# Gated linear attention followed by a ReLU-squared MLP: q loaded for two chunks at a time, scores of two chunks together, sixteen output tiles stored late

## The chip, the cores and the metric

The kernel runs on one core of a Trainium2 chip (trn2). The metric is device time in microseconds (us) of one execution; for the kernel before it is the median of three runs. A profile of one further execution gives the durations. "The span" is the time from the first to the last instruction in that profile; the execution's own time is a little longer.

## The reference

Four sequences of 768 tokens, eight heads of 48 channels. For each head a 48x48 state decays by a gate per channel and gains one outer product per token; the result of the attention, 3,072 tokens of 384 channels, goes through a two-layer MLP with 2,048 hidden units.

```python
for t in range(S):
    state = alpha[:, :, t, :, None] * state + np.einsum('bhd,bhe->bhde', k[:, :, t], v[:, :, t])
    y[:, :, t] = np.einsum('bhd,bhde->bhe', q[:, :, t], state)
x = y.transpose(0, 2, 1, 3).reshape(B * S, H * D)
h = x @ w_in
g = np.maximum(h, 0.0) ** 2
return g @ w_out
```

q, k, v, alpha and the weights come as fp32 in HBM, the output goes back as fp32. The matmuls take bf16 operands.

## The kernel before, in words

**Chunks.** The 3,072 tokens are cut into 24 chunks of 128 (six for each sequence). A chunk's tokens stand on the 128 partitions. Within a chunk the recurrence becomes matrix products: the logarithm of alpha is summed along the tokens by a matmul with a triangular matrix (`e_p0`, L428, and for its transpose `e_pT`, L444), exps of the sum and of its negative scale q and k, and the scores k·q are masked with a triangle (`e_sm`, L558) and multiplied with v (`e_p3b`, L595). The state of the chunks before enters by `e_p3a` (L589), and is brought up to date by `e_ps` and `e_stm` (L567, L579). The result of a chunk, cast to `xn` (L608), is transposed into `xT_big` (L231), either on TensorE (`e_p4`) or, for chunks 18 to 22 (`XTURN`, L313), by a DMA transpose (L620).

**Two ways to q and k.** Up to chunk 10, q and k are scaled on VectorE in their own layout and transposed on TensorE (`e_p1q`, `e_p1k`). From chunk `RAW` = 11 on (L312), POOL casts q and k to bf16 (`e_rb`, L411), a DMA transpose on SP's queue turns each (`e_turn`, L415), the cumulated gate is made in transposed form (`e_pT`), and VectorE multiplies the two (`e_qAT`, `e_kiT`, L506 and L509).

**Scores.** `e_p2` (L549) issues eight matmuls for a chunk. Each contracts over 64 rows (a head's 48 channels, padded), so that two of them, on the upper and the lower 64 rows of the array, stand side by side. They write the two banks of PSUM of the pool `ps_sc`.

**Banks.** PSUM's other banks are five single-bank pools, `sl_bank`. The attention takes turns on the first two (`GLA_BANKS`), the MLP on the others.

**MLP.** `add_moe1` (L652) multiplies groups of one to four token tiles with w_in; ScalarE takes the ReLU, VectorE the square. `add_moe2` (L725) multiplies one tile of 128 tokens with w_out; ScalarE or VectorE copies the result out of PSUM, and a DMA stores it. The last tile goes in two halves of 192 columns (`add_last`, L691).

**Stores.** Tiles 0 to 7 (`HELD` = 8, L644) are copied into two tiles of four (`KEEP`) and stored from SP's queue not before 150 us of the plan, four tiles in one DMA (L763). Tiles 8 to 17 are stored from POOL's queue as they are made (`POOL_OUT`, L643), tiles 18 to 23 from SP's (L772, L721). A token tile's store writes 128 consecutive rows of 1,536 bytes in HBM.

**What sets the order.** Nothing is ordered by hand: class `Plan` (L59) simulates all engines with a cost and a priority for each operation before the program is emitted, and each engine then gets its instructions in the order of the planned starts. DMAs on SP's queue are part of it (`DMA` for loads, `TR` for DMA transposes, `OUT` for stores). A gate (L836) lets chunk s begin when s is at most `LEAD` = 3.7 plus the number of tiles that the MLP has done.

**Loads.** One DMA for each of q, k, v and alpha of a chunk (L371); a token of one head is 48 fp32 numbers, so that every contiguous piece in HBM is 192 bytes. The alphas of the first four chunks come together, four tokens per partition (L336).

Of the kernel before, what the change touches and what calls it, by code (L numbers as in the profile page):

```python
# [38 lines left out]
class Op:  # L39


    def __init__(self, eng, dur, emit, deps=(), prio=0.0, takes=None, gives=None, lat=None, at=0.0):
        self.eng, self.dur, self.emit = eng, dur, emit
        self.deps = []
        for d in deps:
            if d is not None:
                d = d if isinstance(d, tuple) else (d, None)
                if d[0] is not None:
                    self.deps.append(d)
        self.prio = prio  # L50
        self.takes, self.gives, self.lat, self.at = takes, gives, lat, at
        self.start = self.done = None
# [6 lines left out]
class Plan:  # L59
# [13 lines left out]
    def ready(self, op):  # L73
        t = op.at
        slack = PE_SLACK if "PE" in op.durs else 0.0
        if slack and self.free.get("PE", 0.0) > PE_CALM:
            slack = 0.25
        for d, x in op.deps:
            if d.done is None:
                return None  # L80
            if x is None:
                t = max(t, d.done + (slack if d.eng != "PE" else 0.0))
            else:
                t = max(t, d.start + d.dur + x)
        if op.takes is not None:
            best = None
            for sl in op.takes:
                f = sl.free_at()
                if f is not None and (best is None or f < best):
                    best, op.slot = f, sl  # L90
            if best is None:
                return None
            t = max(t, best)
        return t

    def run(self, gate):
        free = self.free
        while any(self.pending.values()):
# [34 lines left out]
            if op.takes is not None:  # L133
                self.ready(op)
                op.slot.release.append(op.gives if op.gives is not None else op)
            self.order.append(op)
# [5 lines left out]
def kernel(  # L142
# [27 lines left out]
    out_r = out.rearrange("(tt p) n -> tt p n", p=P)  # L170

# [26 lines left out]
    nc.gpsimd.tensor_copy(utri_b[:, 0, :], utri_f)  # L198
    JN, JP = 4, 32
# [31 lines left out]
    xT_big = big.tile([P, KT, n_tok], BF16)  # L231
# [80 lines left out]
    RAW = 11  # L312
    XTURN = (18, 23)  # L313
    TLD, TLAT, TLATE = 1.0, 4.0, 2.0
# [3 lines left out]
    def raw_tiles():  # L318
        if R:
            return  # L320
        R["b"] = stage.tile([P, NR, 2, H, DP], BF16, name="rawb", tag="stage")
        nc.gpsimd.memset(R["b"][:, :, :, :, D:], 0.0)
        R["t"] = stage.tile([P, NR, 2, NP, P], BF16, name="rawt", tag="stage")
        R["i"] = stage.tile([P, 2, NP, P], BF16, name="aiT", tag="stage")
# [39 lines left out]
    def add_load(s, nm):  # L364
        d = C[s]
        b, c = divmod(s, NCH)

        def ld():
            if nm not in d:
                d[nm] = loads.tile([P, H, D], FP32, name=nm)  # L370
            pin(nc.sync.dma_start(out=d[nm], in_=SRC[nm][b, c]))  # L371
        prev = C[s - LB].get("use_" + nm) if s >= LB else None
        d["ld_" + nm] = add("DMA", LD if s < 4 else LD1, ld, prev, lat=2.0 if s < 4 else LAG if s < 6 else 2.4, at=0.6)

    def add_chunk(s):
        d = C[s]
# [31 lines left out]
        if raw:  # L408
            w, wz = s % NR, s % 2

            def e_rb(j, nm):  # L411
                raw_tiles()
                pin(nc.gpsimd.tensor_copy(R["b"][:, w, j, :, 0:D], d[nm]))  # L413

            def e_turn(j):  # L415
                pin(nc.sync.dma_start_transpose(out=R["t"][:, w, j], in_=R["b"][:, w, j].rearrange("p h d -> p (h d)")))
            rt = []
            for j, nm in enumerate(["qt", "kt"]):
                cb = add("POOL", 0.55, lambda j=j, nm=nm: e_rb(j, nm), d["ld_" + nm],
                         *([C[s - NR]["turn"][j]] if s >= RAW + NR else []), prio=-5.0)  # L420
                d["use_" + nm] = cb
                t_ = add("TR", TLD, lambda j=j: e_turn(j), cb, *([C[s - NR]["turned"][j]] if s >= RAW + NR else []), lat=TLAT)
                t_.late = TLATE
                rt.append(t_)
            d["turn"] = rt
# [23 lines left out]
        def e_AT():  # L449
            d["qkT"] = work.tile([P, 2 * NP, P], BF16, name="qkT")  # L450
            pin(nc.scalar.activation(d["qkT"][:, NP:2 * NP, :], d["pmT"], AF.Exp))  # L451
# [26 lines left out]
        if raw:  # L478
# [10 lines left out]
            pT.gives = aiT  # L489
            if not last:  # L490
# [15 lines left out]
        def e_qAT():  # L506
            pin(nc.vector.tensor_mul(d["qkT"][:, 0:NP, :], R["t"][:, w, 0], d["qkT"][:, NP:2 * NP, :]))

        def e_kiT():  # L509
            pin(nc.vector.tensor_mul(d["qkT"][:, NP:2 * NP, :], R["t"][:, w, 1], R["i"][:, wz]))  # L510
        if raw:
            if not last:
                mk = d["use_kt"] = add("DVE", 0.47, e_kI, ai, d["ld_kt"], old, **g)
            cp = add("DVE", 0.34, e_qAT, aT, rt[0], **g)
            cpk = add("DVE", 0.34, e_kiT, aiT, rt[1], cp, **g)
            d["turned"] = [cp, cpk]
        else:
            mq = d["use_qt"] = add("DVE", 0.47, e_qA, a_, d["ld_qt"], old, **g)
            mk = d["use_kt"] = add("DVE", 0.47, e_kI, ai, d["ld_kt"], old, **g)

# [28 lines left out]
        def e_p2():  # L549
            sc = d["sc"] = ps_sc.tile([P, 2, NP, P], FP32, name="sc")  # L550
            t = d["qkT"]
            for p in range(NP):
                for hh in range(2):
                    sl = slice(64 * hh, 64 * hh + 64)
                    mm(sc[:, hh, p, :], lhsT=t[sl, NP + p, :], rhs=t[sl, p, :], start=True, stop=True)
        p2 = d["p2"] = plan.add(Op("PE", 0.42, e_p2, [cp, cpk], takes=[sl_sc], lat=0.10, **g))

        def e_sm(hh):  # L558
            if hh == 0:
                d["sm"] = work.tile([P, 2, NP, P], BF16, name="sm")  # L560
            pin(nc.vector.tensor_mul(d["sm"][:, hh], d["sc"][:, hh], utri_b.to_broadcast([P, NP, P])))  # L561
        sm0 = add("DVE", 0.6, lambda: e_sm(0), p2, **g)
        sm1 = add("DVE", 0.6, lambda: e_sm(1), p2, after(sm0), **g)
        p2.gives = sm1

# [52 lines left out]
        if XTURN[0] <= s < XTURN[1]:  # L618
            def e_xt():
                pin(nc.sync.dma_start_transpose(out=xT_big[:, :, s * P:(s + 1) * P], in_=d["xn"]))  # L620
# [6 lines left out]
        def e_xT():  # L627
            cast(xT, xT_big[:, :, s * P:(s + 1) * P], d["px"])
# [15 lines left out]
    HELD, HELD_AT = 8, 150.0  # L644
# [7 lines left out]
    def add_moe1(g, f0, before, lo=0, hi=None, per=1):  # L652
        hi = GN[g] if hi is None else hi
        t0, n = (GT[g] + lo) * P, (hi - lo) * P
# [36 lines left out]
    def add_last(g, tt, before, pools):  # L691
# [3 lines left out]
        for hf in range(2):  # L695
# [24 lines left out]
            def e_out(box=box, cols=cols):  # L720
                pin(nc.sync.dma_start(out=out_r[t][:, cols], in_=box["ob"]))  # L721
# [3 lines left out]
    def add_moe2(g, tt, before, box, quarters, pools):  # L725
# [22 lines left out]
        def e_ev():  # L748
            if held:
                if t % 4 == 0:  # L750
                    KEEP[t // 4] = stage.tile([P, 4, d_model], FP32, name="keep", tag="stage")
# [10 lines left out]
        def e_held():  # L762
            pin(nc.sync.dma_start(out=out_r[t - 3:t + 1].rearrange("t p n -> p t n"), in_=KEEP[t // 4]))  # L763
        if held:
            held_ev.append(ev)
            if t % 4 == 3:
                add("OUT", 2.2, e_held, *held_ev[-4:], at=HELD_AT)
            return op

        def e_out():  # L770
            dma = nc.gpsimd if pool_out else nc.sync
            pin(dma.dma_start(out=out_r[GT[g] + tt], in_=box["ob"]))  # L772
# [61 lines left out]
    LEAD = 3.7  # L834

    def gate(op):  # L836
        s = getattr(op, "gla", None)
        if s is not None:
            return s <= LEAD + (prog["m1"] + prog["m2"]) / 5.12
# [61 lines left out]
```

## Time and profile before

| | |
|---|---|
| median of three runs | 184.71 us (184.2 to 185.06) |
| the profiled execution | 185.07 us |
| its span in the profile | 183.4 us |
| TensorE busy | 177.5 us in 1,908 matmuls |
| VectorE, ScalarE busy | 127.1 us, 126.5 us |
| DMA packets | 120,200, of which 112,400 under 512 bytes |
| read from and written to HBM | 25.17 MB, 4.72 MB |

A line of the page's fifth part gives a group of like instructions: source line, engine, operation, result <- operands, shape, count, then busy time and the mean of one in ns, then the idle time of the engine just ahead of them and what ended it. PE is TensorE's matmuls, PEld its weight loads, DVE VectorE, ACT ScalarE, POOL GpSimd, SP the engine whose queue issues most DMAs. All `mm` calls have line 240 and all PE transposes line 243, so that they are told apart by the names of their tiles: `sc` are the scores, `st` the state. A matmul's listed duration includes its way through the array; how fast matmuls follow one another is read from the starts.

### The profile page before, as it was taken

Reading aid. Unit: us, or ns where it says so; the run is one execution under the profiler, and the core shown is the slowest. Engines: PE = TensorE matmul, PEld = TensorE weight load, DVE = VectorE, ACT = ScalarE, POOL = GpSimd, SP = SyncE. Lnnn points to the kernel's source line nnn. Section 1 sums busy time; section 2 is a strip of 40 time slices with the busy share of each in tenths; the row PEclk is TensorE's granted clock in tenths of the full one; section 3 lists DMA queues with packets and bytes.
Section 4 is the critical chain, followed back from the end, with each engine's and each line's share of the span. In section 5 each row is a group of like instructions: output and inputs, shape, how many; then the busy total and the mean of one; then the engine's idle time right before and its main releaser. Section 6 shows DMA issues by size and latency. Waiting matters only on the chain.

```text
span 183.4 us, 4946 instructions
## 1 busy us (share of the span) xinstructions
PE 177.5 (97%) x1908; PEld 130.5 (71%) x1908; DVE 127.1 (69%) x273; ACT 126.5 (69%) x286; POOL 39.4 (21%) x80
## 2 busy tenths in 40 slices
PE   7999999899999999999999998999999999999993
PEld 2577884567769877867768776667766777778663
DVE  1179898684999998778877867748855984744200
ACT  3677799226859996966967859847975895767321
POOL 8221100021131142132223133342323512000000
PEclk9999999999999999999999999999999999999999
DMA  5999999999999999998999599898898898901022
GB/s 168 215 212 252 302 366 321 326 220 204 177 191 201 194 179 173 141 190 161 150 193 202 113 240 186 161 227 162 170 201 182 176 163 194 301 13 43 12 77 86
DMA packets 120200, 34.12 MB, mean 186 GB/s; under 512 B 112400, under 2 KB 118928, under 8 KB 120176
## 3 DMA queue, kind: packets, MB, share of 16 engines
q1 hardware_dynamic: 119536, 31.83, 80.7%
q0 software_dynamic: 640, 1.97, 3.2%
q8 instruction: 15, 0.25, 0.6%
q14 instruction: 9, 0.07, 0.2%
HBM read 25.17 MB, written 4.72 MB: 163 GB/s over the span
## 4 chain that ended last, share of the span: by engine, by line
PE 49%; DMA 2%; ACT 1%; issue 0%; DVE 0%
PE bank L240 45%; DMA at<-in_alpha_dram 2%; PE sc L240 2%; PE st L240 1%; PE bank L243 1%; ACT aiT L454 0%; ACT r L676 0%; ACT ob L758 0%; ACT L_s L396 0%; ACT ob L716 0%; DVE xT_big L388 0%; ACT qkT L451 0%
## 5 line engine op out<-in xcount | busy, mean ns | idle before, releaser
L240 PE MATMUL bank<-xT_big,w_in_b 128*128 128x256 bf16 (+2 forms) x636 | 76.6, 262 | 0.9 <-ACT r L676 0.7
L240 PE MATMUL bank<-w_out_b,gT 128*128 128x384 bf16 (+1 forms) x400 | 71.6, 320 | 0.5 <-DVE w_out_b L296 0.5
L676 ACT ACTIVATE r<-bank 128x512 bf16<-128x512 f32 x96 | 56.6, 606 | 11.3 <-PE bank L240 9.9
L240 PEld LDWEIGHTS <-w_in_b 128*128 128x128 bf16 x636 | 52.7, 98 | 10.6 <-issue 1.5
L240 PEld LDWEIGHTS <-gT 128*128 128x128 bf16 x416 | 37.2, 98 | 18.7 <-DVE w_out_b L296 1.0
L684 DVE TENSOR_TENSOR gT<-r 128x512 bf16<-128x512 bf16 x96 | 41.8, 453 | 10.2 <-ACT r L676 9.0
L561 DVE TENSOR_TENSOR sm<-sc,utri_b 128x512 bf16<-128x512 f32 x48 | 30.8, 684 | 5.9 <-PE sc L240 5.7
L405 POOL CAST vb<-vt 128x384 bf16<-128x384 f32 x24 | 13.6, 569 | 69.1 <-DMA vt<-in_v_dram 55.2
L386 ACT CAST xn<-bank 128x384 bf16<-128x384 f32 x24 | 11.6, 482 | 11.6 <-PE bank L240 11.5
L505 DVE TENSOR_TENSOR kI_s<-kt,Ainv 128x384 bf16<-128x384 f32 x21 | 12.8, 611 | 7.8 <-ACT Ainv L466 7.8
L240 PEld LDWEIGHTS <-qkT 64*128 64x128 bf16 (+1 forms) x272 | 10.7, 95 | 6.4 <-issue 2.4
L586 ACT CAST sb<-st 128x384 bf16<-128x384 f32 x20 | 9.6, 482 | 7.7 <-DVE st L581 7.5
L758 ACT COPY ob<-bank 128x384 f32<-128x384 f32 x14 | 6.7, 480 | 8.0 <-PE bank L240 8.0
L396 ACT ACTIVATE L_s<-at 128x384 bf16<-128x384 f32 x20 | 10.5, 527 | 2.4 <-DMA at<-in_alpha_dram 2.3
L240 PE MATMUL bank<-warm 128*128 128x256 bf16 (+1 forms) x54 | 10.9, 348 | 1.3 <-DVE warm L188 1.3
L502 DVE TENSOR_TENSOR qA_s<-qt,A 128x384 bf16<-128x384 f32 x11 | 6.3, 575 | 8.0 <-ACT A L462 8.0
L413 POOL CAST rawb<-qt 128x384 bf16<-128x384 f32 x13 | 7.4, 570 | 20.3 <-DMA qt<-in_q_dram 20.3
L413 POOL CAST rawb<-kt 128x384 bf16<-128x384 f32 x13 | 7.6, 587 | 19.0 <-DMA kt<-in_k_dram 11.1
L581 DVE TENSOR_TENSOR st<-st,ae_s 128x384 f32<-128x384 f32 x20 | 11.1, 556 | 0.5 <-PE st L240 0.5
L466 ACT ACTIVATE Ainv<-bank 128x384 bf16<-128x384 f32 x21 | 10.5, 501 | 1.1 <-PE bank L240 1.0
L240 PE MATMUL sc<-qkT 64*128 64x128 bf16 x192 | 9.5, 219 | 0.0
L240 PEld LDWEIGHTS <-sm 128*128 128x128 bf16 x192 | 8.1, 96 | 1.7 <-issue 0.2
(64 smaller groups left out, 165.7 us busy)
## 6 DMA issues: line engine op xcount, KB each, us to landing
qt<-in_q_dram SPq DMA_DIRECT2D x24, 192.0 KB, 4.0
kt<-in_k_dram SPq DMA_DIRECT2D x24, 192.0 KB, 3.6
vt<-in_v_dram SPq DMA_DIRECT2D x24, 192.0 KB, 3.8
at<-in_alpha_dram SPq DMA_DIRECT2D x20, 192.0 KB, 4.0
wo<-in_moe_w_out_dram SPq DMA_DIRECT2D x4, 768.0 KB, 8.5
out_dram<-ob POOLq DMA_DIRECT2D x10, 192.0 KB, 3.1
wi<-in_moe_w_in_dram SPq DMA_DIRECT2D x4, 384.0 KB, 5.3
wi<-in_moe_w_in_dram SPq DMA_DIRECT2D x2, 768.0 KB, 8.3
```

The lines of the kernel that those rows point to most:

```text
L240: pin(nc.tensor.matmul(*a, **kw))
L386: pin(nc.scalar.copy(out_t, in_t))
L396: pin(nc.scalar.activation(L[:, :, 0:D], d["at"], AF.Ln))
L405: pin(nc.gpsimd.tensor_copy(d["vb"], d["vt"]))
L413: pin(nc.gpsimd.tensor_copy(R["b"][:, w, j, :, 0:D], d[nm]))
L466: pin(nc.scalar.activation(d["Ai"], d["pm"][:, 0:HD].rearrange("p (h d) -> p h d", h=H), AF.Exp, scale=-1.0))
L505: pin(nc.vector.tensor_mul(kI[:, :, 0:D], d["kt"], d["Ai"]))
L561: pin(nc.vector.tensor_mul(d["sm"][:, hh], d["sc"][:, hh], utri_b.to_broadcast([P, NP, P])))
L581: pin(nc.vector.tensor_mul(st4, st4, bcast(ae, D)))
L586: pin(nc.scalar.copy(d["sbt"], d["st"]))
L676: pin(nc.scalar.activation(box["r"][:, 0:w], box["ph"][:, 0:w], AF.Relu))
L684: pin(nc.vector.tensor_mul(gT[g][:, f0:f0 + per, lo * P:lo * P + n], r, r))
```

## The change

- **q for two chunks.** From chunk 10 on (`RAW` = 10, even), one DMA loads q of two chunks: partition p holds tokens 2p and 2p + 1 of 256, so that a contiguous piece in HBM is 384 bytes. POOL casts the even and the odd tokens apart, and two DMA transposes turn them. A chunk's q, and with it its scores' columns, its result and its output tile, are then in the order "even tokens, odd tokens": the exp that scales q writes in this order, the mask `utri_q` has its columns in this order, and the store of an output tile from tile 10 on writes to HBM through the access pattern r, i, n (two runs of 64 rows, each row two rows on from the one before). k and v keep their order.
- **Scores of two chunks.** From chunk 10 on (`DUO`), the chunks of a pair have their sixteen score matmuls in one operation, which waits for both. The first chunk's scores go to the two banks of `GLA_BANKS`, which the operation holds until the mask products have read them; the second's go to `ps_sc`. What follows the scores is moved behind (`add_tail`). The gate has a lead of 4.0 for the even and 4.6 for the odd chunk of a pair.
- **Late stores.** Tiles 0 to 15 are held (`HELD` = 16): 0 to 3, 4 to 7 and 8 to 9 go in one DMA each, 10 to 15 one by one, all from SP's queue and none planned before 150 us. POOL's queue keeps tiles 16 and 17.
- **Room.** `xT_big` becomes a ring of twelve tiles; the tiles for q, k and the exp in transposed form are cut anew.

The diff, shortened:

```diff
+    out_q = out.rearrange("(tt i r) n -> tt r i n", i=DP, r=2)
+
+    def rows(t):
+        return out_q[t] if t >= RAW else out_r[t]
...
+    utri_q = consts.tile([P, 1, P], BF16)
+    nc.gpsimd.tensor_copy(utri_q[:, 0, :].rearrange("p (r i) -> p r i", r=2), utri_f.rearrange("p (i r) -> p r i", r=2))
...
-    xT_big = big.tile([P, KT, n_tok], BF16)
+    XR = 12
+    xT_big = big.tile([P, KT, XR * P], BF16)
+    q_s = big.tile([P, 3, 2 * HD], FP32)
...
-    RAW = 11
+    RAW = 10
+    DUO = 10
...
+    def add_q_pair(s):
+        b, c = divmod(s, NCH)
+        src = q[b, :, c * P:(c + 2) * P, :].rearrange("h (p r) d -> p h (r d)", r=2)
+        Q = q_s[:, s // 2 % 3, :].rearrange("p (h rd) -> p h rd", h=H)
+        w = s // 2 % 2
...
+        ld = d["ld_qt"] = add("DMA", 1.6, lambda: pin(nc.sync.dma_start(out=Q, in_=src)), *old, lat=2.4, at=0.6)
+
+        def e_rb(r):
+            raw_tiles()
+            pin(nc.gpsimd.tensor_copy(R["qb"][:, w, r, :, 0:D], Q.rearrange("p h (r d) -> p h r d", r=2)[:, :, r, :]))
+
+        def e_turn(r):
+            pin(nc.sync.dma_start_transpose(out=R["qt"][:, w, r], in_=R["qb"][:, w, r].rearrange("p h d -> p (h d)")))
...
     def add_chunk(s):
+        tail = add_head(s)
+        if s < DUO:
+            add_scores(s)
+            tail()
+        elif s % 2 == 0:
+            tails.append(tail)
+        else:
+            add_scores(s - 1, s)
+            tails.pop()()
+            tail()
...
+        def dst(s):
+            d = C[s]
+            if len(pair) == 2 and s == pair[0]:
+                d["sc"] = [banks[sl.bank].tile([P, NP, P], FP32, name=f"bank{sl.bank}") for sl in GLA_BANKS]
+            else:
+                t = ps_sc.tile([P, 2, NP, P], FP32, name="sc")
+                d["sc"] = [t[:, hh] for hh in range(2)]
+
+        def e_p2():
+            for s in pair:
+                dst(s)
+                t = C[s]["qkT"]
+                for p in range(NP):
+                    for hh in range(2):
+                        sl = slice(64 * hh, 64 * hh + 64)
+                        mm(C[s]["sc"][hh][:, p, :], lhsT=t[sl, NP + p, :], rhs=t[sl, p, :], start=True, stop=True)
+
+        mask = utri_q if pair[0] >= RAW else utri_b
...
         def e_AT():
             d["qkT"] = work.tile([P, 2 * NP, P], BF16, name="qkT")
-            pin(nc.scalar.activation(d["qkT"][:, NP:2 * NP, :], d["pmT"], AF.Exp))
+            pin(nc.scalar.activation(d["qkT"][:, NP:2 * NP, :].rearrange("p n (r i) -> p n r i", r=2),
+                                     d["pmT"].rearrange("p n (i r) -> p n r i", r=2), AF.Exp))
...
         def e_qAT():
-            pin(nc.vector.tensor_mul(d["qkT"][:, 0:NP, :], R["t"][:, w, 0], d["qkT"][:, NP:2 * NP, :]))
+            t = R["qt"][:, s // 2 % 2, :, :, s % 2 * 64:(s % 2 + 1) * 64].rearrange("p r n i -> p n r i")
+            m = d["qkT"].rearrange("p n (r i) -> p n r i", r=2)
+            pin(nc.vector.tensor_mul(m[:, 0:NP], t, m[:, NP:2 * NP]))
...
-    HELD, HELD_AT = 8, 150.0
+    HELD, HELD_AT = 16, 150.0
...
-                pin(nc.sync.dma_start(out=out_r[t][:, cols], in_=box["ob"]))
+                pin(nc.sync.dma_start(out=rows(t)[..., cols], in_=box["ob"]))
...
-        def e_held():
-            pin(nc.sync.dma_start(out=out_r[t - 3:t + 1].rearrange("t p n -> p t n"), in_=KEEP[t // 4]))
+        def e_held(lo, n):
+            k = KEEP[lo // 4][:, lo % 4:lo % 4 + n, :]
+            dst = rows(lo) if n == 1 else out_r[lo:lo + n].rearrange("t p n -> p t n")
+            pin(nc.sync.dma_start(out=dst, in_=k[:, 0, :] if n == 1 else k))
         if held:
             held_ev.append(ev)
             if t % 4 == 3:
-                add("OUT", 2.2, e_held, *held_ev[-4:], at=HELD_AT)
+                n = [x for x in (4, 2, 1) if t - 3 + x <= RAW][0] if t - 3 < RAW else 1
+                lo = t - 3
+                while lo <= t:
+                    m = min(n, 4) if lo < RAW else 1
+                    add("OUT", 0.55 * m, lambda lo=lo, m=m: e_held(lo, m), *held_ev[lo:lo + m], at=HELD_AT)
+                    lo += m
             return op
...
-            pin(dma.dma_start(out=out_r[GT[g] + tt], in_=box["ob"]))
+            pin(dma.dma_start(out=rows(GT[g] + tt), in_=box["ob"]))
...
     LEAD = 3.7
+    DUO_LEAD = 4.0, 4.6
 
     def gate(op):
         s = getattr(op, "gla", None)
         if s is not None:
-            return s <= LEAD + (prog["m1"] + prog["m2"]) / 5.12
+            return s <= (LEAD if s < DUO else DUO_LEAD[s % 2]) + (prog["m1"] + prog["m2"]) / 5.12
         return True
```

## The prediction

> **What bounds the kernel now.** I began with the page's busy times and its 40 slices. TensorE (PE) is busy nearly all the time, the matmul clock is fully granted in every slice, and the 16 DMA engines are full until about 160 us and then nearly idle.
>
> ```profile
> PE 177.5 (97%) x1908; PEld 130.5 (71%) x1908; DVE 127.1 (69%) x273; ACT 126.5 (69%) x286; POOL 39.4 (21%) x80
> ...
> DMA  5999999999999999998999599898898898901022
> ```
>
> Next, the windows (columns: stretch, length, busy time of PE, PEld, DVE, ACT and POOL with instruction counts, clock, DMA share, GB/s). The last 22 us need PE and hardly any DMA. Between 155 and 158 us, when only the held stores move, all engines are full at 365 GB/s. From 174 to 175 us a single 192 KB store moves.
>
> ```profile
> 100.00:150.00 50.00, 49.33 (x507) 36.33 (x506) 35.83 (x76) 38.17 (x91) 16.01 (x29) 1.00 0.88 183
> 162.00:184.00 22.00, 18.48 (x148) 13.58 (x145) 4.47 (x11) 8.01 (x16) 0.00 (x0) 1.00 0.13 45
> ```
> ```profile
> 155.00:158.00 3.00, 3.00 (x28) 2.45 (x26) 1.70 (x4) 2.78 (x6) 0.00 (x0) 1.00 1.04 365
> ...
> 174.00:175.00 1.00, 1.00 (x8) 0.61 (x7) 0.00 (x0) 0.00 (x0) 0.00 (x0) 1.00 0.53 197
> ```
>
> Third, PE's timeline around one scores group (start, length, instruction). Six 256-column matmuls take 0.65 us from 97.82 to the next start; the same six ahead of the scores take 0.75 (96.56 to 97.31). The eight score matmuls take 0.33 us to the next start, while inside the group a pair of 64-row tiles starts every 56 ns, 0.23 in all. So each group loses about 0.095 us entering and 0.097 leaving.
>
> ```profile
> 96.56 0.82 PE L240 MATMUL bank<-xT_big,w_in_b 128*128 128x256 bf16 x6
> 97.31 0.40 PE L240 MATMUL sc<-qkT 64*128 64x128 bf16 x8
> 97.64 0.34 PE L240 MATMUL st<-vb,kI_s 128*128 128x96 bf16 x4
> 97.82 0.82 PE L240 MATMUL bank<-xT_big,w_in_b 128*128 128x256 bf16 x6
> 98.47 0.33 PE L240 MATMUL bank<-sb,qkT 128*128 128x96 bf16 x4
> ```
>
> PE therefore sets the end, and the last store follows it. SP's timeline and the DMA issues show how stores leave.
>
> ```profile
> 152.98 1.12 SPq L763 DMA_DIRECT2D out_dram<-keep  x2
> 155.12 1.97 SPq L620 DMA_TRANSPOSE xT_big<-xn  x1
> 159.15 19.57 SPq L772 DMA_DIRECT2D out_dram<-ob  x5
> ```
> ```profile
> q0 software_dynamic: 640, 1.97, 3.2%
> ...
> out_dram<-keep SPq DMA_DIRECT2D x2, 768.0 KB, 5.1
> out_dram<-ob SPq DMA_DIRECT2D x5, 192.0 KB, 1.9
> ```
>
> **Scores of two chunks back to back.** Chunks 10 to 23 make seven pairs, so seven of 24 groups join their neighbour: 7 x 0.192 = -1.35 us on PE, which is on the path. Each pair now waits for both chunks' qkT. Behind that wait on PE stands whatever the static order put there, mostly MoE matmuls; the gate of 4.0 and 4.6 lets the odd chunk start 0.9 of a tile earlier, about 5 us at 5.2 us of MoE matmuls per tile. The first chunk's scores now take PSUM banks 0 and 1 until two mask products are done (2 x 0.684 = 1.4 us), and four products follow one another on VectorE (2.7 us). Bounds: nothing if MoE fills PE, 1.4 us per pair (10 us) if nothing does. PE idled 0.75 of 90 us between 60 and 150 us, so I take nothing.
>
> **RAW from 11 to 10.** Chunk 10 loses eight transposes (56 ns between starts) and four one-column matmuls (25) and gains four 128-column ones (56): -0.32 us of PE. VectorE trades qA 0.575 and a copy 0.685 for two products, 0.461 + 0.435; ScalarE swaps A (0.494) for two exps (0.612 + 0.625). SP issues two more transposes (1.2 to 2 us each), POOL two more casts (0.57). All of it lies beside PE.
>
> **One q load per pair.** Seven of the 24 q issues go from SP (0.57 us each, -4 us), and 1,024 packets of 384 B replace 2,048 of 192. A 192-byte packet takes 17.5 ns by the window from 60 to 100 us (175 GB/s over 16 engines, 0.98 busy), a 1,536-byte row 66. Bounds for 384 B: 17.5 and 35; near the first, 21. That frees about 0.9 us of DMA per pair. It shortens no PE path but the one long stall, 0.8 us of PE at 111 us behind a late alpha load; with mid-kernel stores gone as well I take -0.5.
>
> **New strides.** The exp writes permuted and reads PSUM in steps of two; the q product walks runs of 64. Nearest rows: 612 and 461 ns as now. Upper bounds: the exp at double, 14 x 0.6 = 8.6 us of ScalarE; the product at the fp32 mask product's 684, 3.1 us of VectorE. Both engines are 69% busy, and MoE covers them: nothing. If that cover went, the pairs would be late, as in the second rival. The extra mask cast (0.28 us) delays POOL's tri until about 3.8 us; PE first reads it at 6.9.
>
> **Late stores.** POOL loses eight stores (0.54 each). SP issues nine held stores, five of tiles 18 to 22 and two halves: 16 for nine, 0.33 to 0.57 each, after its last load. Sixteen tiles of 128 rows on 16 engines cost 16 x 0.53 = 8.5 us of DMA from 153 us; tiles 0 to 7 cost 4.2 now. The window after 162 has 20 us of DMA to spare. The last xn transpose queues behind them: it landed 5.2 us after 155.1, and PE reads it at 163.3.
>
> **The disputed price: stores of tiles 10 to 23.** Their DRAM side becomes r, i, n: two runs of 64 rows, the row index outermost no longer 128. Lower bound: 0.53 us, the store as now. For the upper bound I look at how a store is dealt out. POOL's ten stores left 640 packets, 64 each for 128 rows; in the trace's packet list these are 32 of 4,608 B, 16 of 3,072 B and 16 of 4 B. That is 16 shares of 4,608 + 4,608 + 3,072 = 12,288 B, eight consecutive rows: the deal follows the outermost index in equal blocks. Every transfer of before has 128 there on both sides. With two values there, equal blocks are two shares of 64 rows, and a store takes 64 x 66 ns = 4.2 us of two engines. Is 66 ns an engine's own pace? The single store at 174 us (0.53 for eight rows) and the crowd at 155 to 158 (365/16 GB/s, 67 ns) agree, so yes. By its shape the nearest row is the store as now; by how it is dealt, the two shares. I take 4.2: a deal in equal blocks of an index of two cannot give sixteen.
>
> The Trainium skill says the same more directly (DMA: Bandwidth & Descriptors, section Why a DMA increments its semaphore by 16 and not by 1): a DMA uses the largest engine count up to 16 that divides the slowest dimension of both access patterns, which would be 2 here. By that rule a store costs 4.2 us, without it 0.53; no run here shows it yet.
>
> **The sum.** Both engines get everything in SP's order: ten tiles (0 to 9) from 152.98 at 0.53 end at 158.3; six held singles, 6 x 4.22 = 25.3, at 183.6; tiles 18 to 22, 21.1, at 204.7; two halves of 768 B rows (36 ns: 64 x 36 = 2.3), 4.6, at 209.3; the queued transpose adds 0.5. From the last packets (182.1 in the packet list) to the end of the span 1.3 us: 211.1. The profiled execution took 185.07 for a span of 183.4, 1.67 around it: 212.8. That execution lies 0.36 above the median of the three runs, 184.71: **212.5 us**. PE's gains vanish in this, since PE ends near 180 and the stores near 210. Even were the last transpose caught behind four slow stores (17 us), PE would end near 190, ahead of its stores' turn.
>
> **Rivals.**
> - *All stores stay on 16 engines.* Then PE decides: 185.07 - 1.35 - 0.32 - 0.5 = 182.9. For it: the bytes and rows are unchanged and DMA is idle after 162 us. Against: the block deal above. Span of this case 181.9 to 184.
> - *Sixteen engines, but pairs starve PE.* Place: banks 0 and 1 and VectorE around each pair. It loses once a pair's wait passes 0.3 us on average (2.1 against -2.17 gained); at 0.9 per pair the time is 189. For it: 2.7 us of products in a row. Against: 0.75 us of idle PE in 90.
> - *Nothing measurable:* the sixteen-engine case with its gain eaten, 184 to 185.6.
>
> **How the numbers follow.** Chances: two shares 0.56, sixteen and faster 0.33, sixteen and no difference 0.04, sixteen with starved pairs 0.07. The two-share case alone is 207 to 216 (two engines alone up to 10% quicker per row; the mean of 70 ns, four above the median, adds 3 us). The range must reach the second case: 182 to 216. Faster by over 0.5% 0.33, within 0.5% (about what a measurement of this kernel can tell from no change) 0.04, slower 0.63.
>
> **What would show it.** Two shares: after 162 us a flat DMA share near 2/16 at some 45 GB/s, PE done near 180 and the span ending on out_dram; single stores landing in over 4 us. Sixteen shares: those stores land in 2 us and DMA is idle from 165. Switches: pieces of sixteen score matmuls of 0.55 us to the next start instead of two of 0.33. The forecast is wrong if single stores of tiles 10 to 15 land in about 2 us.

## The result and the profile after

The changed kernel takes **218.27 us** (median of six runs, 215.94 to 221.07) where the kernel before takes 184.88 in the same comparison (six runs, 184.2 to 186.25). The ratio is 1.177 (95% interval 1.169 to 1.184). The forecast was 212.5, with a range to 216; against the 184.71 that it started from this is 27.8 us more, and the measured effect is 33.4. The profiled execution took 218.79 us for a span of 217.1. A median here is of all runs of a kernel, while a ratio leaves out those over 1.5% above the fastest of their kernel (221.07 here, one of 359.37 in half_nox).

First the page (busy times, then the clock and DMA rows of the 40 slices, 5.4 us each). TensorE does nearly the same work as before (1,900 matmuls for 1,908) in the first 34 slices, and then nothing. From there on the DMA row shows one tenth, less in the last slice, and the clock that TensorE is granted falls to half once it has nothing to do.

```profile
PE 175.9 (81%) x1900; PEld 130.1 (60%) x1900; DVE 123.4 (57%) x271; ACT 127.6 (59%) x289; POOL 36.1 (17%) x76
...
PEclk9999999999999999999999999999999999755555
DMA  6999999798997797979688787794545211111110
```

The windows (stretch, length, busy time and count of PE, PEld, DVE, ACT and POOL, clock, DMA share, GB/s) say it in numbers. From 184 to the end the DMA engines are 0.12 busy, which is two of sixteen, and move 46 GB/s. Before, PE lost 0.67 us in the window from 100 to 150; now it loses 2.1.

```profile
100.00:150.00 50.00, 47.90 (x514) 35.80 (x512) 34.76 (x75) 38.01 (x91) 12.74 (x24) 1.00 0.84 165
...
162.00:184.00 22.00, 22.00 (x169) 15.73 (x166) 3.41 (x8) 7.96 (x15) 0.80 (x1) 1.00 0.29 93
184.00:218.00 34.00, 0.24 (x3) 0.01 (x1) 0.00 (x0) 0.32 (x1) 0.00 (x0) 0.54 0.12 46
```

SP's timeline (start, length, instruction, count) shows how the stores leave. One held DMA goes at 152.66. Then SP stands before the DMA transpose of chunk 22, whose input is not ready, until 159.15, and the other eight held DMAs stand behind it. From there the stores follow one another at about 4 us: the five of `ob` take 18.61 us to issue.

```profile
152.66 0.57 SPq L857 DMA_DIRECT2D out_dram<-keep  x1
159.15 1.18 SPq L712 DMA_TRANSPOSE xT_big<-xn  x1
160.38 20.74 SPq L857 DMA_DIRECT2D out_dram<-keep  x8
181.23 18.61 SPq L871 DMA_DIRECT2D out_dram<-ob  x5
199.94 8.68 SPq L813 DMA_DIRECT2D out_dram<-ob  x2
```

PE's timeline (start, length, instruction, and in brackets the idle time before it with what ended it) holds a pair of score groups, the wait ahead of it, and PE's end. Between the two groups of this pair PE steps on without a loss: 155.85 to 156.08 is 0.23 us, the length that eight score matmuls have inside a group. So it is in five of the seven pairs; in the first two PE stops inside the pair until the second chunk's `qkT` comes, for 0.20 and 1.01 us (the first line is the longer stop). The last matmul ends at 171.04 + 13.20 = 184.24, against 180.48 before.

```profile
89.44 0.40 PE L256 MATMUL sc<-qkT 64*128 64x128 bf16 x8 [1.01 <-DVE qkT L613]
...
153.79 2.13 PE L256 MATMUL bank<-xT_big,w_in_b 128*128 128x256 bf16 x18 [1.23 <-DMA xT_big<-xn]
155.85 0.40 PE L256 MATMUL bank<-qkT 64*128 64x128 bf16 x8
156.08 0.39 PE L256 MATMUL sc<-qkT 64*128 64x128 bf16 x8
156.40 1.16 PE L256 MATMUL bank<-xT_big,w_in_b 128*128 128x256 bf16 x9
...
171.04 13.20 PE L256 MATMUL bank<-w_out_b,gT 128*128 128x384 bf16 x96
```

In the trace's packet list, 65 packets of 1,536 B start in every 2 us from 176 us on, and each further store of 128 rows ends 3.92 us after the one before. A packet is listed with 65 ns, but with 64 rows on each of two engines the next one starts after 3.92 / 64 = 61 ns.

### The profile page after: what moved, and what is told of

Its sections match the earlier page's. It is cut to its first block, busy times and chain, and to the rows that moved or that the text cites. A ratio compares the mean times of both kernels' runs of the same rounds, so it can differ in the third digit from the quotient of the medians.

```text
span 217.1 us, 4892 instructions
## 1 busy us (share of the span) xinstructions
PE 175.9 (81%) x1900; PEld 130.1 (60%) x1900; DVE 123.4 (57%) x271; ACT 127.6 (59%) x289; POOL 36.1 (17%) x76
## 4 chain that ended last, share of the span: by engine, by line
PE 52%; DMA 24%; ACT 5%; SPq 3%; POOL 2%; issue 2%; DVE 1%; POOLq 0%; ACTq 0%; DVEq 0%
PE bank L256 48%; DMA out_dram<-ob 7%; DMA vt<-in_v_dram 5%; DMA at<-in_alpha_dram 4%; DMA rawt<-rawb 3%; DMA xT_big<-xn 3%; DMA kt<-in_k_dram 3%; PE bank L259 2%; SPq L404 2%; ACT r L768 2%; SPq L422 1%; PE sc L256 1%; POOL vb L509 1%; PE st L256 1%; ACT xn L490 1%
## 5 line engine op out<-in xcount | busy, mean ns | idle before, releaser
L256 PE MATMUL bank<-xT_big,w_in_b 128*128 128x256 bf16 (+2 forms) x636 | 74.2, 263 | 3.5 <-DMA xT_big<-xn 3.3
L256 PE MATMUL bank<-w_out_b,gT 128*128 128x384 bf16 (+1 forms) x400 | 70.8, 320 | 0.5 <-DVE w_out_b L312 0.5
L776 DVE TENSOR_TENSOR gT<-r 128x512 bf16<-128x512 bf16 x96 | 39.7, 437 | 15.8 <-ACT r L768 14.9
L606 DVE TENSOR_TENSOR kI_s<-kt,Ainv 128x384 bf16<-128x384 f32 x21 | 12.1, 574 | 7.3 <-ACT Ainv L566 7.3
L468 DVE TENSOR_TENSOR sm<-sc,utri_b 128x512 bf16<-128x512 f32 x20 | 12.8, 681 | 1.1 <-PE sc L256 1.0
L419 POOL CAST rawb<-q_s 128x384 bf16<-128x384 f32 x14 | 7.2, 544 | 32.2 <-DMA q_s<-in_q_dram 32.2
L850 ACT COPY keep<-bank 128x384 f32<-128x384 f32 x14 | 6.7, 478 | 7.6 <-PE bank L256 7.5
L603 DVE TENSOR_TENSOR qA_s<-q_s,A 128x384 bf16<-128x384 f32 x10 | 6.1, 611 | 8.8 <-ACT A L562 8.8
L850 ACT COPY ob<-bank 128x384 f32<-128x384 f32 x7 | 3.3, 478 | 11.5 <-PE bank L256 11.4
L468 DVE TENSOR_TENSOR sm<-bank,utri_q 128x512 bf16<-128x512 f32 x14 | 9.0, 683 | 0.1
```

What stands on the lines that cost most here:

```text
L256: pin(nc.tensor.matmul(*a, **kw))
L468: pin(nc.vector.tensor_mul(d["sm"][:, hh], d["sc"][hh], mask.to_broadcast([P, NP, P])))
L606: pin(nc.vector.tensor_mul(kI[:, :, 0:D], d["kt"], d["Ai"]))
L776: pin(nc.vector.tensor_mul(gT[g][:, f0:f0 + per, lo * P:lo * P + n], r, r))
L850: pin(nc.scalar.copy(box["ob"], box["po"]))
```

## The experiments

**Theory:** the access pattern r, i, n gives a store two engines, and a queue of such stores sets the end. **Rivals:** the rows themselves (every other one) are slow; the number of stores held to the end is the cause; the pairs or the q loads cost the time. A second question came up with the first results: why the change gains nothing even with full-width stores.

### Row order left out: natural

The stores go to consecutive rows, so the output's rows stand in another order.

```diff
-        return out_q[t] if t >= RAW else out_r[t]
+        return out_r[t]
```


> The changed kernel, but tiles 10 to 23 are stored with the plain pattern of 128 consecutive rows (so the tokens of a pair of chunks lie in HBM in the order even, odd: the order of rows is left out). Number, size and moment of the stores stay. Theory (the store is dealt out along the outermost index of its HBM side, two shares for r, i, n): the stores use 16 engines again, the queue of stores is gone by 165 us, and PE's end decides: 184.2 as in the changed kernel, plus 4.6 as in the kernel before (180.5 to 185.1) = 188.8 us. Rivals: if pairs that starve PE or the late holding of sixteen tiles cost the 33 us, it stays at about 218.

Measured 186.63 against 183.87, ratio 1.015 (1.011 to 1.019). The pattern is the cause of 30 of the 33 us. What is left is a loss, not the gain that the sixteen-engine rival had forecast.

### The same values in two DMAs per tile: half

```diff
+            for r in range(2):
+                pin(eng.dma_start(out=out_q[t, r][:, cols], in_=src[64 * r:64 * r + 64]))
```


> The changed kernel, but each tile from 10 on is stored by two DMAs of 64 partitions, one for the even and one for the odd rows; the same bytes go to the same places as in the changed kernel. Outermost index is 64 then. Theory: 16 engines, 188.8 us, perhaps 0.5 more for the second issue of the last store. Rival (rows that lie two apart in HBM are slow to write by themselves): about 218.

Measured 187.67, ratio 1.021 (1.015 to 1.027). Each DMA now has 64 as its outermost count on both sides. The list of DMA issues (count, KB each, median us to landing) has the held halves, and those of tiles 18 to 22, landing within 3 us, although every row still lies two rows from the next one.

```profile
out_dram<-keep SPq DMA_DIRECT2D x12, 96.0 KB, 2.9
out_dram<-ob SPq DMA_DIRECT2D x10, 96.0 KB, 2.2
```

### Other outermost counts: r16 and r4

The rows are split into 16 runs of 8 (rows 16 apart) and 4 runs of 32 (rows 4 apart); both store rows to other places.

```diff
-    out_q = out.rearrange("(tt i r) n -> tt r i n", i=DP, r=2)
+    out_q = out.rearrange("(tt i r) n -> tt r i n", i=8, r=16)   # r16
+    out_q = out.rearrange("(tt i r) n -> tt r i n", i=32, r=4)   # r4
```


> The changed kernel with the store's pattern cut as sixteen runs of eight rows, each row sixteen on from the one before (the order of rows in HBM is then not that of the reference). One DMA per tile, rows still scattered, outermost index 16. Theory: sixteen shares of eight rows, 188.8 us. Rival (scattered rows are slow): about 218 or more.

> The changed kernel with the store's pattern cut as four runs of 32 rows, each row four on from the one before (rows in another order than the reference's). Theory (as many engines as the outermost index counts): 32 x 65 ns = 2.1 us a store on four engines, eleven stores from 164.2 us to 187, two halves of 1.2 to 189.5, 3.0 to the end: 190 to 192.5 us. Rival (any count under 16 falls back to two engines): 218; rival (any count but two uses all): 187.

r16: 187.2, ratio 1.018 (1.013 to 1.022). r4: 193.22 against 184.06, ratio 1.042 (1.037 to 1.047), which is 191.8 us and within what was expected. Rows that lie even farther apart cost no more with 16 outermost than in natural and half, and four outermost give a time between. In r4's window from 172 to 188 the DMA engines are 0.27 busy, 4.3 of sixteen, and move twice what two engines did.

```profile
172.00:188.00 16.00, 10.50 (x81) 7.17 (x78) 0.00 (x0) 2.55 (x6) 0.00 (x0) 0.95 0.27 101
```

The packets of POOL's two stores show the deal itself. In the changed kernel a store leaves 42 packets of 4,608 B and two of 1,536, which is two shares of 21 x 4,608 + 1,536 B, 64 rows each. In r4 it is four shares of 10 x 4,608 + 3,072, 32 rows each; in natural and r16 sixteen of 8 rows; in half sixteen of 4 rows for each DMA of 64.

So the outermost count decides: 2 gives two shares, 4 gives four, 16, 64 and 128 give sixteen.

### The pattern alone in the kernel before: before_q, before_q18

The store pattern is put into the kernel before, from tile 10 or from tile 18 on; those rows are in another order.

```diff
+        return out_q[t] if t >= 10 else out_r[t]     # before_q18: t >= 18
...
-            pin(dma.dma_start(out=out_r[GT[g] + tt], in_=box["ob"]))
+            pin(dma.dma_start(out=rows(GT[g] + tt), in_=box["ob"]))
```


> The kernel before, with nothing changed but the pattern of the stores of tiles 10 to 23, which is that of the changed kernel (so rows lie in another order than the reference's). Theory: from the end of tile 19's copy (168 us) the two engines take 4.2 us a tile: 168.5 to 172.7, 173.2 to 177.4, 181.6, 185.8, then the halves 2.3 each, 190.4, and 3.0 to the end of the execution: 193.4 us. The stores of tiles 10 to 17 from POOL's queue go in between and may slow loads; up to 197 if SP's two engines fall behind by 150 us. Rival (pairs or late holding cost the time, the pattern nothing): 184.9.

> The kernel before, with the changed store pattern on tiles 18 to 23 alone, those from SP's queue at the end (rows in another order than the reference's); POOL's stores in mid-kernel keep the plain pattern. Theory (price 4.2 us a store on two engines, nothing else): tile 19's store from 168.3 to 172.5, then 177.7, 181.9, 186.1, two halves to 190.7 and 3.0 to the end: 193.7 us, where all fourteen tiles gave 214. Then the other 20 us are two-engine stores amid the loads. Rival (each scattered store costs the same wherever it is: six of fourteen): 184 + 6/14 of 30 = 197.

before_q: 214.09 against 183.87, ratio 1.163 (1.159 to 1.167), **20 us beyond what was expected**. before_q18: 193.61 against 184.34, ratio 1.050 (1.044 to 1.056), as expected to 0.1 us. Its SP timeline has the five stores and the two halves in 25 us:

```profile
158.68 19.75 SPq L776 DMA_DIRECT2D out_dram<-ob  x5
179.07 4.70 SPq L725 DMA_DIRECT2D out_dram<-ob  x2
```

The two kernels differ only in tiles 10 to 17, which POOL stores in mid-kernel: (214.09 - 183.87) - (193.61 - 184.34), about 21 us for eight stores that nothing waits for. In before_q, SP's timeline has transposes, otherwise 1.2 us each, standing for up to 8 us. (The profiled execution took 221.0 us, 7 above the median, so these lines show the kind of delay and not its usual size.)

```profile
126.22 7.75 SPq L420 DMA_TRANSPOSE rawt<-rawb  x1
...
161.69 8.34 SPq L420 DMA_TRANSPOSE rawt<-rawb  x2
```

In the changed kernel none of these stores is under way before 150 us. There the pattern costs about as much, 30 us by natural, but as a queue at the end.

### Where the missing 6 us lie: after_x22, after_x22_p

In after_x22 chunk 22's result is transposed on TensorE, so that SP has no transpose between its stores; after_x22_p also stores POOL's tiles 16 and 17 to consecutive rows (their rows are in another order).

```diff
-    XTURN = (18, 23)
+    XTURN = (18, 22)
...
+        return out_q[t] if t >= RAW and t not in (16, 17) else out_r[t]     # after_x22_p alone
```


> The changed kernel, but chunk 22's result is transposed on TensorE and not by a DMA, so that no transpose stands in SP's order between the held stores (in the changed kernel it waits for its xn until 159 us, with eight of the nine held stores behind it). All slow stores stay. Theory: what the forecast mis-sized is the moment at which the chain of two-engine stores begins, 158 us in the forecast against 164 in the changed kernel; without the transpose the held stores leave from about 152.7 us and the time falls by about 6, to 212. Rival (the 6 us are slower packets, contention or PE's later end): it stays near 218.

> The kernel after_x22 with tiles 16 and 17, the two that leave from POOL's queue, stored with the plain pattern (their rows in another order than the reference's). In after_x22 the chain of two-engine stores began at 159.3 us, five earlier than in the changed kernel, but its packets of 1,536 B came at 15 to 42 per 2 us instead of 65 while POOL's two stores moved, and the time fell by only 2. Theory (POOL's scattered stores use one or both of the same engines, and the forecast left them out): with plain ones the chain runs undisturbed, 159.3 + 11 x 4.16 + 4.6 = 209.7, and 3.0 to the end of the execution: 212.7 us. Rival (what was lost lies elsewhere): 216 as in after_x22.

after_x22: 216.29 against 184.34, ratio 1.174 (1.166 to 1.181): at most a third of the 6 us, and by the ratios not to be told from the change's 1.177. SP now issues all nine held DMAs from 152.94, but takes 26.51 us for them. POOL's two stores, issued at 154.17 and 167.25, now both fall among the held ones. While the first one's packets move, until 165 us, SP's 1,536-byte packets drop to 15 (162 to 164 us) and 30 (to 166) in 2 us instead of 65; beside the second they keep 65 at first and drop to 42 near its end. after_x22_p: 213.0 against 185.43, ratio 1.148 (1.140 to 1.155), as expected, and its nine take 22.00:

```profile
152.94 26.51 SPq L857 DMA_DIRECT2D out_dram<-keep  x9
```
```profile
153.81 22.00 SPq L857 DMA_DIRECT2D out_dram<-keep  x9
175.94 19.19 SPq L871 DMA_DIRECT2D out_dram<-ob  x5
```

Its profiled span is 211.6 us; the forecast's was 211.1. So the transpose and POOL's stores together are what the forecast's total missed. That the two spans agree so closely is partly luck, though: in the packet list of after_x22_p tiles 0 to 9 are done at 161.5, 3.2 us later than forecast, and eleven stores at 3.92 take 3.3 us less than at 4.22.

### Why full-width stores don't gain: half_nox, half_single, pairs_nox

In half, PE waits once for the DMA transposes of two results. PE's timeline, then SP's, then the windows (clock in the third column from the right):

```profile
134.98 0.81 PE L260 MATMUL bank<-w_out_b,gT 128*128 128x384 bf16 x4
138.35 2.74 PE L260 MATMUL bank<-xT_big,w_in_b 128*128 128x256 bf16 x12 [2.55 <-DMA xT_big<-xn]
140.88 1.13 PE L260 MATMUL bank<-w_out_b,gT 128*128 128x384 bf16 x4
```
```profile
130.44 1.21 SPq L524 DMA_TRANSPOSE aiT<-aiT  x1
...
132.38 1.20 SPq L524 DMA_TRANSPOSE rawt<-rawb  x1
133.68 3.51 SPq L716 DMA_TRANSPOSE xT_big<-xn  x2
```
```profile
135.00:138.20 3.20, 0.80 (x7) 0.28 (x4) 1.78 (x4) 2.56 (x7) 0.00 (x0) 0.98 0.30 58
138.20:141.70 3.50, 3.35 (x16) 2.19 (x16) 0.43 (x1) 1.54 (x3) 0.61 (x2) 0.53 1.02 216
```

ScalarE wrote the two `xn` at 128.80 and 130.20, 1.4 us apart; both then stood behind SP's other transposes, and their own took until 137.2. After the wait the clock is 0.53: twelve matmuls take 140.88 - 138.35 = 2.53 us where 12 x 0.109 = 1.31 is usual, and the next four 1.06 where 0.65 is. The wait costs 2.55 and the slow clock 1.6.

half_nox is half with all results transposed on TensorE (`XTURN = (0, 0)`); half_single is half with scores chunk by chunk (`DUO = 99`, with which every chunk's gate has the lead of 3.7 again), the q loads still paired; pairs_nox stores consecutive rows and loads q chunk by chunk, scores still paired. In spite of its label, and of what its text says, pairs_nox has the DMA transposes of results (`XTURN` as in the change).

```diff
-    XTURN = (18, 23)
+    XTURN = (0, 0)          # half_nox
-    DUO = 10
+    DUO = 99                # half_single
-        ld = d["ld_qt"] = add("DMA", 1.6, lambda: pin(nc.sync.dma_start(out=Q, in_=src)), *old, lat=2.4, at=0.6)
+        lds = [add("DMA", 1.0, lambda r=r: pin(nc.sync.dma_start(out=Q4[:, :, r, :], in_=SRC["qt"][b, c + r])), *old, lat=2.4, at=0.6) for r in range(2)]     # pairs_nox
```


> The changed kernel with two stores of 64 rows per tile (16 engines) and with no result transposed by a DMA: chunks 18 to 22 go over TensorE like the others. The kernel with the two stores alone took 187.7, and its PE waited 2.6 us at 135 us for the DMA transposes of a pair and then ran 3.4 us at half clock, some 1.7 lost. Theory (the pairs bring both results of a pair late to SP's queue): without them 4.3 less, 0.84 more for fifteen transposes of 56 ns: 184.2. Rival (pairs starve PE in other places as well, through banks 0 and 1 or the mask products): 186 or more.

> The changed kernel with two stores of 64 rows per tile, but scores of one chunk at a time (the q loads stay paired, DMA transposes of results stay). Theory: the wait at 135 us comes of pairs and goes (-4.3), seven switches come back (+1.35): 184.7. Rival (the wait comes of the paired q load and its two transposes, not of the scores): 189.

> Pairs of scores alone: the changed kernel with q loaded chunk by chunk in its own order (so no permuted exp, mask or store; stores of tiles 10 to 15 still one by one, sixteen held), DMA transposes of chunks 18 to 22 as in the changed kernel. What the pairing of q loads adds: if it mattered for PE (its two transposes wait for one another), the wait at 135 us shrinks and the time is 184 to 185; if the wait is that of both results of a pair on SP's queue, it stays, and the time is that of natural, 186.6.

half_nox: 185.74 against 184.34, ratio 1.006 (1.002 to 1.010). The wait and the slow clock are gone (mean clock 0.999), and PE ends at 179.9, 0.6 before the kernel before; but 4.3 us lie between PE's end and the span's, against 2.9. The last tile now leaves in four DMAs of 64 rows, one behind the other on SP.

half_single: 189.35, ratio 1.025 (1.018 to 1.033). Here the theory that the paired scores alone make the wait **fell**: without them PE's waits are as long, and spread over more places. The time is that of the rival, which blamed the paired q load. In its list of PE's waits (total, times, longest):

```profile
PE sc L260 <- DVE qkT L617: 2.1, 3, 1.2
...
PE bank L260 <- ACT r L772: 1.2, 2, 1.0
PE bank L260 <- DMA xT_big<-xn: 1.1, 1, 1.1
```

pairs_nox: 188.65 against 185.43, ratio 1.015 (1.008 to 1.022), the same as natural's 1.015: with paired scores it makes no difference whether q is loaded for one chunk or two. A wait for `xT_big` is there with either (2.2 us), though at 151 us instead of 135. So neither the paired scores nor the paired q load is needed for a loss of this size; half_nox shows that most of it goes with the DMA transposes of the results.

### Last tile, and stores in mid-kernel: half_nox_act, pairs_h8

half_nox_act is half_nox with the odd rows of the last tile stored from ScalarE's queue. pairs_h8 is pairs_nox's kernel without DMA transposes of results and with eight tiles held instead of sixteen.

```diff
+                for r, eng in enumerate([nc.sync, nc.scalar]):     # half_nox_act
...
-    HELD, HELD_AT = 16, 150.0
+    HELD, HELD_AT = 8, 150.0                                       # pairs_h8
```


> The kernel half_nox with the odd rows of the last token tile stored from ScalarE's queue instead of SP's. In half_nox PE ended at 179.9 us (180.5 in the kernel before), but the span went on for 4.3 us, against 2.9 before: four stores of 64 rows follow one another on SP at 0.55 us each. Theory (the tail is SP's issue time): 1.1 us less, 184.6. Rival (two stores for a tile cost the tail in another way, landing or the end of the program): 185.7.

> Pairs of scores with q chunk by chunk, no result transposed by a DMA, and eight tiles held instead of sixteen (tiles 8 to 17 from POOL's queue as in the kernel before, in the plain order). Theory: PE ends at 179.9 as in half_nox or a little later, the tail is the 2.9 us of the kernel before, 184.5 less what the kernel before's chip gives: 0.6 below the kernel before. Rival (late holding is what makes room for the loads; without it DMA is full and PE waits): 0.5 or more above the kernel before.

half_nox_act: 186.67 against 185.43, ratio 1.007 (1.003 to 1.012), not to be told from half_nox: inconclusive. (In the profiled execution the tail is 3.7 us instead of 4.3.) pairs_h8: 187.51 against 185.43, ratio 1.012 (1.006 to 1.019); the expected small gain is excluded, and the sign is the rival's. Whether that is owed to the stores in mid-kernel alone stays open, since no kernel differs from it in that one thing.

### The change with its stores mended: tailplain, tailplain_x

tailplain is half_nox with q of the last two chunks in its own order, so that the last two tiles are stored in single DMAs of 128 rows; tailplain_x adds DMA transposes of the results of chunks 20 and 21. Both compute the reference's values.

```diff
+        if t < RAW or t >= 22:
+            pin(eng.dma_start(out=out_r[t][:, cols], in_=src))
...
-    XTURN = (18, 23)
+    XTURN = (0, 0)          # tailplain_x: (20, 22)
```


> The kernel half_nox with q of the last two chunks (22 and 23) loaded chunk by chunk in its own order, so that the last two tiles are stored plainly, one DMA of 128 rows or half tile. Same values and places as the reference's. Theory: what kept half_nox (PE's end 179.9) from beating the kernel before (180.5) is the tail of doubled stores on SP, 4.3 against 2.9 us; with plain ones 1.4 less, so 0.5 below the kernel before, ratio 0.995 to 1.0. Rival (the extra loads of 192-byte packets make the last pair late): 1.01.

> tailplain with the results of chunks 20 and 21 transposed by DMAs again, which spares PE six transposes (0.34 us). Theory (both results of a pair reach SP's queue together, behind transposes of q and k, and PE needs them 4 to 5 us later): PE waits some 1 to 3 us at 150 us, ratio 1.005 to 1.015. Rival (only the pair of 18 and 19 was caught so): 0.993.

tailplain: 184.06 against 184.06, ratio 1.002 (0.999 to 1.005), which excludes the expected gain of 0.5 us. tailplain_x: 183.77, ratio 1.000 (0.998 to 1.002), which is neither what the theory nor what the rival expected: two transposes, at this place, cost nothing that can be measured. In its list of PE's waits `xT_big` is missing, and there are 0.8 us for `qkT` at a pair, which the kernel before doesn't have:

```profile
PE sc L260 <- DVE qkT L501: 0.8, 1, 0.8
```

tailplain_x's PE ends at 179.7, 0.8 earlier than before, and its span is 183.0 against 183.4. Mended, the change makes no difference that can be measured; no version here beats the kernel before.

## Why the prediction was right or wrong

**Right: what decides and its price.** The likeliest case came, by the mechanism named: two shares of 64 rows. A store takes 3.92 us (forecast 4.22, and quicker by up to 10% was allowed for); before_q18 came out at its expected time; the flat DMA share of 0.12 and 46 GB/s after PE's end is the sign that the prediction had asked for. What it argued from POOL's packets, a deal of the outermost index in equal parts, is shown by r4, r16, half and the change itself, in the packets of POOL's stores and in the times. The Trainium skill's rule (DMA: Bandwidth & Descriptors, section Why a DMA increments its semaphore by 16 and not by 1), the largest count up to 16 that divides the slowest dimension of both patterns, agrees: 2 gave two shares, 4 gave four (4.3 engines by the DMA share), 16 and 64 gave sixteen.

**Wrong: the start of the chain.** The step that failed is "Both engines get everything in SP's order: ten tiles (0 to 9) from 152.98". It placed the transpose of chunk 22 as 0.5 us within a queue that never stands still. It asked what the transpose loses behind the stores, not what the stores lose behind the transpose. In the changed kernel that transpose is second in SP's order. It waits for the result of the last but one chunk, which the pair finishes 1.0 us ahead of the last one's (in the kernel before 6.5), so SP stood until 159.15 with eight DMAs behind it. Tiles 0 to 9 were done 6.8 us later than forecast. About 3 us of this are there without the transpose as well (after_x22_p, 161.5): SP's queue came to the first store 0.8 us later, its packets came 1.1 us behind the issue, and one of POOL's stores moved in between.

| step | forecast | measured |
|---|---|---|
| held stores start | 152.98, all | 152.66 one, 160.38 the other eight |
| tiles 0 to 9 done | 158.3 | 165.1 |
| price of a store | 4.22 | 3.92 |
| last full rows | 204.7 | 211.3 |
| halves done | 209.3 | 215.5 |
| span | 211.1 | 217.1 |
| PE's end | near 180 | 184.24 |

**Left out: POOL's two stores.** Tiles 16 and 17 have the new pattern too, and go from POOL at 153.0 and 164.2. The sum had them nowhere. The second one's packets move until 173 us, and beside them the chain's second store takes 5.6 us instead of 3.92. With the measured terms the sum is 165.1 for tiles 0 to 9, 1.2 more until both engines keep their pace, eleven stores 43.1, POOL's store 1.7, the halves 4.2 and the end 1.5: 216.8; measured 217.1. In after_x22 both of POOL's stores fall among the held ones and cost 215.2 - 211.6 = 3.6 us of span.

**Luck in the total.** The late start (6.8 us), the slow first store (1.2) and POOL's (1.7) are 9.7 us against the forecast. The price, 0.3 us too high for each of eleven stores, took 3.3 us back, and the halves 0.4. With the forecast's own prices the changed kernel would have missed by about 9 us and not by 6.

**Right: the switches.** In five of seven pairs the step from the first group to the second shows no loss, and PE's busy time fell by 177.5 - 175.9 = 1.6 us, near the 1.35 + 0.32 of the forecast. 384-byte packets take 22 ns (forecast 21). For the pairs' waits the forecast took nothing; PE waited 1.2 us for `qkT` inside the first two pairs here, and 0.2 to 0.9 in the kernels with paired scores that store on sixteen engines, where the kernel before has no such wait.

**Wrong, though it did not decide: the sixteen-engine rival at 182.9.** With all stores on sixteen engines the time is 186.6 to 187.7. The rival took PE's end as 180.48 - 2.17 = 178.3 and the tail as it was. half's PE ends at 182.6: 178.3 + 2.55 of wait + 1.6 of slow clock = 182.5. Its tail is 4.0 us instead of 2.9. The starved pairs that I gave 0.07 were thus the better story for that case, but at another place: not banks or VectorE, but in half both results of a pair reaching SP's queue 1.4 us apart, behind other transposes. That this is what the pairs do is read from half's trace; half_single, without paired scores, waits as long. tailplain_x, without that wait and with the tail mended, has its PE end at 179.7: of the 2.17 expected, 0.5 goes to nine more PE transposes (9 x 56 ns) and 0.8 to a pair's wait for `qkT`. I didn't seek the rest.

**What stays open:** which two engines POOL's stores use, and so why they cost about 2 us in the change and 3.6 in after_x22; why the first store of the chain is 0.8 to 1.2 us slower than the next; and what held stores are worth by themselves.

## What to carry to other kernels

Before a store or load gets a rearranged access pattern, look at its outermost count on both sides: with 2 there a DMA of 128 rows took 3.9 us on two engines, where two DMAs of 64 rows with the same bytes and the same places were not limited so. When a chain is placed on an in-order queue, ask of each instruction in it what it waits for, and move what stands behind. And a gain on the bounding engine counts only once the queue that feeds it (here SP's transposes) and the tail behind it are summed as well.

## What the runs showed of the hardware

**A few narrow DMAs can be dear in mid-kernel.** Eight two-engine stores there cost about 21 us (before_q against before_q18), though nothing waits for them. That loads and transposes wait for their shares on the two busy engines would fit SP's transposes of up to 8 us; it wasn't measured apart.

**TensorE's clock goes by stretches of 3.41 us.** In all 17 profiles the granted clock changes only at whole multiples of 3.41 us after its first record, so that a kernel falls into stretches of this length. Where PE idled for 2.06 us or more of a stretch at full clock, the next one had half clock: 2.06 in r16, 2.29 in natural, 2.30 in half, 2.37 in after_x22, 2.50 in after_x22_p. Where it idled for 1.91 (r4) or less, the next one stayed full. A wait counts by its part within one stretch: the 2.10 us of the change lie across an edge, 1.12 and 0.98, and of pairs_nox's 2.17 us 1.78 lie in one, and neither halved the clock. natural's two stretches, then r4's:

```profile
134.88:138.29 3.41, 1.12 (x9) 0.67 (x8) 1.44 (x4) 2.06 (x6) 0.00 (x0) 1.00 0.28 50
138.29:141.71 3.42, 3.42 (x27) 2.04 (x25) 1.28 (x3) 1.56 (x3) 1.29 (x3) 0.50 1.22 249
```
```profile
135.33:138.75 3.42, 1.50 (x15) 0.93 (x13) 1.88 (x4) 2.03 (x6) 0.00 (x0) 1.00 0.26 48
138.75:142.16 3.41, 3.41 (x47) 2.68 (x45) 2.07 (x5) 1.82 (x4) 1.25 (x3) 1.00 1.20 251
```

The Trainium skill (TensorE: Matmul & The Clock Gate, section Part 1: The HAM clock gate) puts the fall to half rate after at least one idle window of about 3.4 us, and says that the window runs freely. The length of the stretches agrees. That a window must be idle throughout does not: 2.06 us of one was enough here. Between 1.91 and 2.06 no stretch lies, and after a stretch at half clock the bound may be another: in before_q one with 1.12 us of idle time was followed by half clock once more.
